# Softmax exponentials of VectorE placed in ScalarE's score groups, with three score banks on both sides and balanced PV batches

## The chip, the cores and the metric

One Trainium2 chip, one core. The metric is device time in microseconds of one execution of the kernel, as a median of several runs. In the rows, PE is TensorE (matmul), PEld its weight loads, DVE VectorE, ACT ScalarE, POOL GpSimd and SP SyncE, which issues most of the DMAs.

## What is computed

A transformer block with adaptive layer norm, for one sequence of 2048 tokens, width 640, 32 heads of 20, and a hidden width of 1536:

```python
mod = (silu(c) @ w_mod).reshape(1, 6, 1, -1)      # sa, ca, ga, sb, cb, gb
h = layernorm(x) * (1 + ca) + sa
q, k, v = split_heads(h @ wqkv)                    # 32 heads of 20
p = softmax(einsum('bhqd,bhkd->bhqk', q, k) * 20 ** -0.5)
x = x + ga * (merge_heads(einsum('bhqk,bhkd->bhqd', p, v)) @ wo)
h = layernorm(x) * (1 + cb) + sb
x = x + gb * (((h @ w_gate) * (h @ w_up)) @ w_down)
```

The 32 x 2048 x 2048 exponentials of the softmax are by far the most elementwise work.

## The kernel before

The program is planned before it is emitted. Every instruction is a `Task` with an engine, a guessed duration, dependences, a priority and slots to acquire (PSUM banks, SBUF buffers). `Sched.run` plays these tasks through guessed times, and what it picks, in the order it picks it, becomes the fixed order of each engine's queue; `emit_program` writes out the queues with semaphore waits. So a guessed duration (`ps_cost`, `sb_cost`, the numbers in `dve(...)` and `act(...)`) never sets a time on the chip, only the order.

**Units, items, chunks.** The queries are cut into four chunks of 512 (`CHUNKS`), the heads into eight sets of four. A chunk and a set are an item, 32 in all. An item has 64 units: one head of the four (its row strip `s`) times one key tile of 128. A unit's scores are one matmul of 32 rows by 512 columns (L919) into one PSUM bank; matmuls of different `s` run side by side in the four 32-row strips of TensorE.

**Two ways to the exponential.** 1824 units go through ScalarE: consecutive units form a group, alternately three in banks 0 to 2 (`GA`, set A) and two in banks 3 and 4 (`GB`, set B), and one `activation` (L944) takes the whole group to a slot of `PA` or `PB`. 224 units (`QUADS`: one quad of four units an item in the first chunk, two in the others) go through VectorE: the scores land in a bank of the pool `G` (banks 5 and 6), `P1` (L980) adds a bias, clamps at zero and writes int16 that is read as bf16, and five shifted copies of the quad (`SH`, L999) follow; the six versions are summed by the PV matmuls. `DB0` holds `NB0` quads, `DSS` holds `NSS` shifted copies.

**PV.** `pv_issue` writes matmuls of 128 rows by 32 columns (L1307): a unit's values against its exponentials, into the strip `s` of bank 7. A ScalarE unit has one, a VectorE unit six. At the end of an item VectorE transposes bank 7, normalizes, transposes back (L1050 to L1058), and DMAs (L1069) copy the pieces to `Ocp`.

**Other rounds on TensorE (X).** `Round` takes one bank of `G`, runs a chain of matmuls and releases the bank at its evacuation: K, Q and V projections (L738, L770), and for each finished chunk a `suffix`: output projection (op, L1119), layer norm and transposes (h2T, L1151), gate and up (L1191, 24 rounds of five), down (dn, L1221, eight rounds of twelve). `gate(...)` holds each suffix round back until the next chunk's groups have come so far; the last chunk's suffix is the tail. `xck` holds the chunk's residual, so it is reloaded (L1109) after the suffix before has written its output.

**What TensorE takes next** is decided in `pick_pe`: the next score group if its banks are free, with VectorE units' scores behind it when they are ready; then a PV batch of up to ten ScalarE units and whatever VectorE work is ready, from six matmuls on; then a VectorE unit's score by itself; then an X matmul; last a filler matmul, when planned activity in a window of 3.4 us is under `FILL_MIN`. TensorE, like the others, works its queue strictly in the order so found.

Of the kernel before, what the change touches and what calls it, by code (L numbers as in the profile page):

```python
# [55 lines left out]
class Slots:  # L56
# [6 lines left out]
    def avail(self):  # L63
        best = None
        for k, (i, rel) in enumerate(self.free):
            t = 0.0
# [23 lines left out]
class Sched:  # L90
# [83 lines left out]
    def acquire(self, task, t):  # L174
        got = []
        for pool, key, refs in task.acq:
            a = pool.avail()
            if a is None or a[0] > t:
                return False
        for pool, key, refs in task.acq:  # L180
            a = pool.avail()
# [167 lines left out]
SHIFTS = (0, 18, 34, 56, 77, 105)  # L349
SHIFT_GAIN = 3.046480226123085  # L350


def ps_cost(n):
    return n * 1.042 + 110.0
# [6 lines left out]
def build_kernel(nc, A_x, A_wqkv, A_wo, B_x, B_w_gate, B_w_up, B_w_down, c, w_mod, out):  # L361
# [94 lines left out]
    NPS = 4  # L456
    PA = alloc("PA", [128, NPS, 3 * 512], BF16)
    PB = alloc("PB", [128, NPS, 2 * 512], BF16)
    NB0, NSS = 2, 3
# [35 lines left out]
    NSX = 9  # L495
# [4 lines left out]
    GA = [0, 1, 2]  # L500
    GB = [3, 4]
# [4 lines left out]
    pA = Slots(list(range(NPS)), "PA")  # L506
    pB = Slots(list(range(NPS)), "PB")
# [142 lines left out]
    def ln1(tc, prio):  # L650
# [10 lines left out]
        for i in range(4):  # L661
            t = tc * 4 + i
            ags.append(dve(80, lambda e, t=t, i=i: e.bn_aggr(mv[:, t, :], st[:, i, :]), bns[2 * i:2 * i + 2], prio=prio))
# [10 lines left out]
        for i in range(4):  # L674
            t = tc * 4 + i
            t_xn[tc].append(dve(sb_cost(640, .27), lambda e, t=t, i=i: e.tensor_scalar(
                xn[:, s2, i, :], x0[:, t, :], mv[:, t, 0:1], rs[:, t:t + 1], op0=ALU.subtract, op1=ALU.mult),
                [p2] + dps, prio=prio))
# [3 lines left out]
    def hT_rounds(tc, prio):  # L682
# [3 lines left out]
        for k in range(KD):  # L686
# [6 lines left out]
            def after(r, k=k):  # L693
# [7 lines left out]
                return [dve(340, f, [r.last] + ev_col, prio=1)]  # L701
# [82 lines left out]
    units_per_chunk = [NSET * 4 * (NT * n // 512) for (_, n) in CHUNKS]  # L784
    act_units_per_chunk = [u - NSET * 4 * q for u, q in zip(units_per_chunk, QUADS)]
    gpc = [a / 2.5 for a in act_units_per_chunk]
    gstart = [sum(gpc[:i]) for i in range(NC + 1)]
# [78 lines left out]
    items = [(ci, j) for ci in range(NC) for j in range(NSET)]  # L866
    groups = []
    dquads = []
    pvq = []
    item_info = {}  # L870
    ubuf = []
    glist = []

    class Unit:
        __slots__ = ("item", "ci", "j", "s", "kts", "n", "task", "pslot", "off", "pv_ready", "is_d", "quad", "grp")

    for it, (ci, j) in enumerate(items):
        q0, n = CHUNKS[ci]
        rr = 512 // n
        nkg = NT // rr  # L880
        nq = QUADS[ci]
        info = {"pv_total": 0, "pv_done": 0, "acts": [], "quads": []}
        quads = [[] for _ in range(nq)]
        for kg in range(nkg):
            for s in range(4):
                u = Unit()
                u.item, u.ci, u.j, u.s, u.n = it, ci, j, s, n
                u.kts = list(range(kg * rr, kg * rr + rr))
                u.task = None
                u.quad = None  # L890
                q = kg // 4
                u.is_d = q < nq and s == kg % 4
                if u.is_d:
                    quads[q].append(u)
                else:
                    ubuf.append(u)
                    info["acts"].append(u)
        info["quads"] = quads
        for q in quads:
            dquads.append((it, q))  # L900
        item_info[it] = info
    gi_ = 0
    while ubuf:
        k = 3 if gi_ % 2 == 0 else 2
        glist.append(ubuf[:k])
        ubuf = ubuf[k:]
        gi_ += 1
    NG = len(glist)

# [15 lines left out]
    prev_s = [None]  # L925
    act_tasks = []
    for g, us in enumerate(glist):
        even = g % 2 == 0
        bset, banks_, pool_, pbuf = (setA, GA, pA, PA) if even else (setB, GB, pB, PB)
        ems = []  # L930
        deps = []
        for i, u in enumerate(us):
            deps += unit_score_deps(u)
            ems += unit_score_emits(u, (lambda b=banks_[i]: bank(b)))
# [4 lines left out]
        score_q.append((ts, us))  # L939
# [3 lines left out]
        def fexp(e, nu=nu, b0=banks_[0], pbuf=pbuf, cellp=cellp):  # L943
            return e.activation(pbuf[:, cellp["p"], 0:nu * 512],  # L944
                                ps[:, b0:b0 + nu, :].rearrange("p b c -> p (b c)"), AFT.Exp, scale=ESCALE)
        ta = Task("act", nu * 512 / 1.2 + 52.0, fexp, [ts], prio=g, name=f"E{g}")
        ta.acq = [(pool_, "p", nu)]

        def on_e(task, g=g, us=us, bset=bset, pool_=pool_, pbuf=pbuf, cellp=cellp):
            cellp["p"] = task.slots["p"]  # L950
            bset.done(0, task)
            sc.progress = max(sc.progress, g + 1)
            for i, u in enumerate(us):
                u.pslot = (pool_, pbuf, task.slots["p"])
                u.off = i * 512
                u.task = task
        ta.on_start = on_e
        sc.add(ta)
        act_tasks.append(ta)
        for u in us:  # L960
            pvq.append(u)

    st_pv = {"item": 0, "free": [d_pz]}
    dq_units = []
    d_state = {}
    pvd_ready = []
    for qi, (it, us) in enumerate(dquads):
        st_ = {"units": us, "p1": [], "slot": None, "item": it, "pv": [None] * NSH, "left": NSH, "rel": []}
        d_state[qi] = st_
        for x, u in enumerate(us):  # L970
            cell = {}
            ems = unit_score_emits(u, (lambda cell=cell: bank(cell["b"])))
            ts = Task("pe", 216.0, ems, list(dict.fromkeys(unit_score_deps(u))), ctr="pes", mode="S", name=f"D{qi}.{x}")
            ts.acq = [(G, "g", 1)]
            ts.on_start = lambda task, cell=cell: cell.__setitem__("b", task.slots["g"])
            sc.left += 1
            dq_units.append((ts, u, qi, x))

            def fp1(e, cell=cell, st_=st_, x=x):
                return e.tensor_scalar(DB0[:, st_["slot"], x * 512:(x + 1) * 512], bank(cell["b"]), EBIAS, 0.0,  # L980
                                       op0=ALU.add, op1=ALU.max)
            tp = Task("dve", ps_cost(512), fp1, [ts] + wpad[("K", 1)] + wpad[("Q", 1)] + st_["p1"][:1], prio=3.0 + .001 * qi,
                      name=f"P1.{qi}.{x}")
            if x == 0:
                tp.acq = [(sB0, "b0", NSH)]

            def on_p1(task, cell=cell, st_=st_, x=x):
                if x == 0:
                    st_["slot"] = task.slots["b0"]
                G.done(cell["b"], task)  # L990
            tp.on_start = on_p1
            sc.add(tp)
            st_["p1"].append(tp)
        st_["src"] = {0: st_["p1"]}
        for jj in range(1, NSH):
# [4 lines left out]
            tsx = Task("dve", sb_cost(2048, .27), fsh, list(st_["p1"]) + wpad[("K", 1)] + wpad[("Q", 1)], prio=2.5 + .001 * qi, name=f"SH.{qi}.{jj}")  # L1000
# [43 lines left out]
    def item_end_tasks(it):  # L1044
# [5 lines left out]
        t1 = Task("dve", ps_cost(n), lambda e: e.transpose(OT[:, 0:n], ps[:, BPV, 0:n]), [], prio=0.0, name=f"T1.{it}")  # L1050
        t1.acq = [(sOT, "o", 1)]
        item_info[it]["t1"] = t1
        t2 = dve(90, lambda e: e.reciprocal(invT[:, 0:nb32].unsqueeze(2),
# [4 lines left out]
        t4 = dve(sb_cost(n, .55), lambda e: e.transpose(OcT[:, cell["s"], 0:n], OTn[:, 0:n]), [t3], prio=1.5)  # L1058
# [29 lines left out]
    def suffix(ci):  # L1088
# [12 lines left out]
        def gate(w):  # L1101
            g = gb + 9 + int((gl - 9) * 0.985 * rc_[1] / w_tot)
# [11 lines left out]
        for tl in range(ntl):  # L1114
# [21 lines left out]
            ag = dve(85, lambda e, t=t, tl=tl: e.bn_aggr(mv2[:, t, :], st2[:, tl, :]), bn, prio=2.8)  # L1136
# [4 lines left out]
            t_xn2.append(dve(sb_cost(640, .27), lambda e, t=t, tl=tl: e.tensor_scalar(  # L1141
# [6 lines left out]
        for k in range(KD):  # L1148
# [6 lines left out]
            def after(r, k=k):  # L1155
                f = lambda e: e.tensor_scalar(h2T[:, k, 0:n], bankh(r.b["b"])[:, 0:n], mcol[:, 3, k:k + 1],  # L1156
                                              mcol[:, 2, k:k + 1], op0=ALU.mult, op1=ALU.add)
                return [dve(sb_cost(n, .55), f, [r.last, r_sb.evac[0], r_cb.evac[0]] + sfx_done.get("h2T", []) + proj_last,
# [81 lines left out]
    for it in range(len(items)):  # L1240
        ci, j = items[it]
        t1s[it] = item_end_tasks(it)
        if j == NSET - 1:
            sfx_done["qdead"] = [score_q[g][0] for g in range(NG) if any(u.ci == NC - 2 for u in score_q[g][1])][-1:] + \
                [a for (a, u, _, _) in dq_units if u.ci == NC - 2]
# [12 lines left out]
    PVMIN = 6  # L1258
    FILL_MIN = 3000.0
# [11 lines left out]
    def pv_candidates(t, maxn):  # L1271
# [24 lines left out]
        return res  # L1296

# [93 lines left out]
    def pick_pe(t):  # L1391
        sc.pull("pe")
        if pvstate["sidx"] < NG:
            ts, us = score_q[pvstate["sidx"]]
            if acquire_ready(ts, t):
                start = mode_start("S", t)
                dur, used = issue_S(ts, us, t, start)
                pvstate["sidx"] += 1
# [152 lines left out]
```

## Time and profile before

| | us |
|---|---|
| median of 3 runs | 1027.2 (1025.96 to 1028.4) |
| profiled execution | 1028.66 |
| its span, first to last instruction | 1026.6 |
| ScalarE busy / TensorE busy / VectorE busy | 856.0 / 940.6 / 598.8 |
| score matmuls L919, busy | 347.9 |
| VectorE's P1 L980 and shifts L999, busy | 145.2 and 184.6 |

Busy time of a group of instructions is the union of their spans; groups overlap. Matmul spans include the way through the array, so rows of different lines on TensorE add up to more than its busy time. A wait is told with the instruction that waited and the one that released it. In the chain of waits each piece is the work, or the wait, that the end of the kernel hung on at that moment.

### The profile page before, as it was taken

The page shows a single profiled execution, that of the slowest core. Times are in us where ns is not written, and L with a number is a line of the kernel's source. Part 1 is how long each engine was busy: PE and PEld are TensorE (multiplying, and loading weights), DVE is VectorE, ACT ScalarE, POOL GpSimd, SP SyncE. Part 2 cuts the span into 40 slices and gives each one's busy share as a digit, 9 for nine tenths or more (in the row PEclk, how much of TensorE's full clock was granted, in tenths as well). Part 3 has the DMA queues.
Part 4 walks back from the last instruction along what each step waited for, and adds up shares of the span by engine and source line. Part 5 has one row for each costly group of instructions (what it writes and reads, how often), then busy time and mean ns, then how long its engine had stood idle before and what let it go on. Part 6 is the DMA issues. An engine that isn't in the chain of part 4 may idle for free.

```text
span 1026.6 us, 16949 instructions
## 1 busy us (share of the span) xinstructions
PE 940.6 (92%) x7028; PEld 296.3 (29%) x7028; DVE 598.8 (58%) x1055; ACT 856.0 (83%) x758; POOL 57.5 (6%) x69
## 2 busy tenths in 40 slices
PE   2799999999998999999999889999999999999888
PEld 1342322222222222222223222222233322223545
DVE  5865555554459665545555676556466855664432
ACT  3277999999797899989999989899899989999010
POOL 5002000000016000000000010000000000000000
PEclk9899999999897898988899989989899979999989
DMA  9120000000050011110200101111441001111100
GB/s 306 52 65 4 4 4 5 3 2 4 4 145 4 3 42 30 36 24 4 43 17 11 36 5 36 43 30 23 86 85 44 4 23 30 43 37 42 55 1 26
DMA packets 82348, 37.46 MB, mean 36 GB/s; under 512 B 65632, under 2 KB 82272, under 8 KB 82272
## 3 DMA queue, kind: packets, MB, share of 16 engines
q1 hardware_dynamic: 79648, 33.11, 12.5%
q10 hardware_dynamic: 2624, 3.28, 1.0%
q8 instruction: 55, 0.90, 0.4%
q14 instruction: 21, 0.17, 0.1%
HBM read 31.13 MB, written 2.62 MB: 33 GB/s over the span
## 4 chain that ended last, share of the span: by engine, by line
PE 60%; DVE 18%; ACT 16%; issue 3%; POOL 1%; DMA 1%; ACTq 1%; DVEq 0%; POOLq 0%
PE ps_all L919 16%; PE ps_all L1307 13%; PE ps_all L1191 12%; ACT PA L944 9%; PE ps_all L738 8%; ACT PB L944 7%; DVE DSS L999 5%; PE ps_all L1221 4%; DVE DB L980 4%; PE ps_all L770 2%; PE ps_all L1119 2%; DVE st L657 1%; DVE OTn L1055 1%; DVE OT L1050 1%; DVE xck L1125 1%
## 5 line engine op out<-in xcount | busy, mean ns | idle before, releaser
L944 ACT ACTIVATE PA<-ps_all 128x1536 bf16<-128x1536 f32 x365 | 538.9, 1476 | 64.9 <-PE ps_all L919 63.2
L944 ACT ACTIVATE PB<-ps_all 128x1024 bf16<-128x1024 f32 x365 | 383.6, 1051 | 19.1 <-PE ps_all L919 18.6
L919 PE MATMUL ps_all<-QT,KT 32*128 32x512 bf16 x2048 | 347.9, 406 | 34.9 <-DVE DB L980 14.9
L999 DVE TENSOR_SCALAR DSS<-DB 128x2048 int16<-128x2048 int16 x280 | 184.6, 689 | 2.3 <-PE ps_all L1307 1.6
L919 PEld LDWEIGHTS ps_all<-QT,KT 32*128 32x128 bf16 x2048 | 83.5, 91 | 336.1 <-ACT PA L944 102.0
L1307 PE MATMUL ps_all<-PA,Vf 128*32 128x512 bf16 (+1 forms) x1095 | 165.9, 413 | 3.8 <-DVE OT L1050 3.7
L1307 PE MATMUL ps_all<-PB,Vf 128*32 128x512 bf16 (+1 forms) x729 | 160.5, 410 | 0.7 <-DVE OT L1050 0.4
L980 DVE TENSOR_SCALAR DB<-ps_all 128x512 int16<-128x512 f32 x224 | 145.2, 683 | 21.4 <-PE ps_all L919 19.5
L1307 PE MATMUL ps_all<-DSS,Vf 128*32 128x512 bf16 (+1 forms) x1120 | 146.7, 395 | 4.6 <-DVE DSS L999 4.5
L1191 PE MATMUL ps_all<-h2T,stg 128*128 128x512 bf16 x390 | 122.4, 420 | 0.5 <-DVE h2T L1156 0.3
L1206 DVE TENSOR_TENSOR hprod<-ps_all,gsb 128x512 bf16<-128x512 f32 x48 | 33.1, 690 | 82.9 <-PE ps_all L1191 82.9
L1196 DVE CAST gsb<-ps_all 128x512 bf16<-128x512 f32 x36 | 24.8, 690 | 80.1 <-PE ps_all L1191 80.1
L1221 PE MATMUL ps_all<-wd,hprod 128*128 128x320 bf16 x384 | 62.4, 304 | 0.8 <-DVE hprod L1206 0.8
L738 PE MATMUL ps_all<-hT,Wk 128*128 128x512 bf16 x160 | 50.3, 400 | 3.4 <-DVE QT L750 1.5
L1307 PEld LDWEIGHTS ps_all<-PA,Vf 128*32 128x32 bf16 (+1 forms) x1095 | 33.0, 95 | 64.0 <-issue 52.7
L1199 ACT CAST gsb<-ps_all 128x512 bf16<-128x512 f32 x12 | 7.0, 585 | 53.1 <-PE ps_all L1191 53.1
L1227 DVE TENSOR_TENSOR xck<-ps_all,xck 128x320 bf16<-128x320 f32 x32 | 15.6, 488 | 61.1 <-PE ps_all L1221 61.1
L1191 PEld LDWEIGHTS ps_all<-h2T,stg 128*128 128x128 bf16 x390 | 30.1, 101 | 68.5 <-issue 48.9
L738 PE MATMUL ps_all<-hT,Wq 128*128 128x512 bf16 x160 | 48.2, 397 | 0.0
L746 DVE CAST KT<-ps_all 128x512 bf16<-128x512 f32 x32 | 22.0, 688 | 42.2 <-PE ps_all L738 42.1
L750 DVE TENSOR_SCALAR QT<-ps_all 128x512 bf16<-128x512 f32 x32 | 22.1, 690 | 39.2 <-PE ps_all L738 39.2
L1307 PEld LDWEIGHTS ps_all<-PB,Vf 128*32 128x32 bf16 (+1 forms) x729 | 31.1, 95 | 47.3 <-issue 42.1
(69 smaller groups left out, 560.3 us busy)
## 6 DMA issues: line engine op xcount, KB each, us to landing
stg<-in_B_w_gate_dram SPq DMA_DIRECT2D x39, 160.0 KB, 2.4
stg<-in_B_w_up_dram SPq DMA_DIRECT2D x39, 160.0 KB, 2.7
x<-in_A_x_dram SPq DMA_DIRECT2D x4, 640.0 KB
xck<-in_A_x_dram SPq DMA_DIRECT2D x4, 640.0 KB
out_dram<-xck SPq DMA_DIRECT2D x16, 160.0 KB, 1.8
Ocp<-OcT SPq DMA_DIRECT2D x112, 20.0 KB
wd<-in_B_w_down_dram SPq DMA_DIRECT2D x1, 1920.0 KB, 8.9
wm<-in_w_mod_dram ACTq DMA_DIRECT2D x2, 800.0 KB, 8.7
```

The costliest lines, as they stand in the source:

```text
L738: f = lambda e, b, k=k: e.matmul(bank(b), wx[:, k, j, :], hT[:, k, tc * 512:(tc + 1) * 512], start=(k == 0), stop=(k == KD - 1))
L746: f = lambda e: e.tensor_copy(KT[:, j, tc * 512:(tc + 1) * 512], bank(r.b["b"]))
L750: f = lambda e, ci=ci, so=so, n=n: e.tensor_scalar(QT[ci][:, j, :], ps[:, r.b["b"], so:so + n], QSCALE, None, op0=ALU.mult)
L919: ems.append(lambda e, i=i, kt=kt: e.matmul(dstf()[:, i * u.n:(i + 1) * u.n], KT[32 * u.s:32 * u.s + 32, u.j, kt * 128:(kt + 1) * 128], QT ...
L944: return e.activation(pbuf[:, cellp["p"], 0:nu * 512], ps[:, b0:b0 + nu, :].rearrange("p b c -> p (b c)"), AFT.Exp, scale=ESCALE)
L980: return e.tensor_scalar(DB0[:, st_["slot"], x * 512:(x + 1) * 512], bank(cell["b"]), EBIAS, 0.0, op0=ALU.add, op1=ALU.max)
L999: return e.tensor_scalar(DSS[:, cell["s"], :], DB0[:, st_["slot"], :], float(SHIFTS[jj]), None, op0=ALU.add)
L1191: f = lambda e, b, k=k, cell=wbuf[w_]: e.matmul(ps[:, b, 0:n], cell["t"][:, k, :], h2T[:, k, 0:n], start=(k == 0), stop=(k == KD - 1))
L1196: f = lambda e: e.tensor_copy(gsb[:, gs, 0:n], ps[:, r.b["b"], 0:n])
L1206: f = lambda e: e.tensor_tensor(hprod[:, fc, 0:n], ps[:, r.b["b"], 0:n], gsb[:, gs, 0:n], ALU.mult)
L1221: f = lambda e, b, fc=fc, tl=tl, hf=hf: e.matmul(ps[:, b, 0:320], hprod[:, fc, tl * 128:(tl + 1) * 128], wd_sb[:, fc, 320 * hf:320 * hf + ...
L1307: ems.append(lambda e, i=i, kt=kt, stt=stt, stp=stp: e.matmul(ps[32 * s:32 * s + mc, BPV, 0:u.n], Vf[:, (kt * H + 4 * u.j + s) * VW:(kt * ...
```

## The change

1. `glist` is formed anew. Set A stays three banks wide, set B is two wide in the first chunk and three in the last three (`WIDE`), where it takes bank 5 from `G` (`widen`). Where a group is three wide and a VectorE unit is due (`due`, with a lead of `D_LEAD` = 0.35 of an item, and never among the first 18 ScalarE units), the group is two ScalarE units and that VectorE unit, of another row strip. The separate list of VectorE scores (`dq_units`), their place in `pick_pe` and `d_ok` are gone.
2. The bank set of such a group has two holders, the exponential and P1, and is free when both are done. The first unit of a quad makes the score group acquire the `DB0` slot. P1 has priority 0.8 in place of 3.0.
3. `PA` and `PB` (four slots each) become one ring `PP` of eight slots of three units. `NB0` goes from 2 to 3, `NSS` from 3 to 2.
4. `pick_pe`: an X matmul comes ahead of PV when planned activity is low and the ring is not; PV takes up to 24 candidates, cut by `pv_balance` to nearly equal numbers in the four strips, from 8 matmuls on right after a score group and 12 otherwise (or when forced by a low ring or an item's end); then X; then small PV batches.
5. Planner constants: `ps_cost`, the durations of layer norm, evacuations, shifts and transposes; `NSX` 11; `GATE_F` (0.985 for the three gated suffixes, as before). `gstart` and `gpc` are counted from `glist`.

`CHUNKS`, `QUADS` and the `suffix` work are as before. The diff, cut to its core:

```diff
+D_LEAD = 0.35
+NB0, NSS = 3, 2
+NPS = 8
+WIDE = (1, 2, 3)
+PVMIN, PVMAX, PVCAP = 8, 12, 24
...
-    PA = alloc("PA", [128, NPS, 3 * 512], BF16)
-    PB = alloc("PB", [128, NPS, 2 * 512], BF16)
-    NB0, NSS = 2, 3
+    PP = alloc("PP", [128, NPS, 3 * 512], BF16)
...
-    while ubuf:
-        k = 3 if gi_ % 2 == 0 else 2
-        glist.append(ubuf[:k])
...
+    while ap < NA or dp < len(dlist):
+        even = len(glist) % 2 == 0
+        wide = 3 if even or ap >= NA or ubuf[ap].ci in WIDE else 2
+        us = ubuf[ap:ap + wide]
+        d = None
+        if not quad_left and dp < len(dlist):
+            quad_left = dlist[dp:dp + 4]
+        if wide == 3 and quad_left and due[dp] <= ap:
+            two = ubuf[ap:ap + 2]
+            for u in quad_left:
+                if u.s not in [v.s for v in two]:
+                    d, us = u, two
+                    break
...
+        glist.append((us, d, 0 if even else 3, wide))
...
-        ts.acq = [(bset, "b", 1)]
+        ts.acq = [(bset, "b", 1 if du is None else 2)]
+        if g in widen:
+            ts.acq.append((G, "g5", 1, 5))
...
+            if du.first:
+                ts.acq.append((sB0, "b0", NSH))
...
+            tp = Task("dve", ps_cost(512), fp1, [ts] + wpad[("K", 1)] + wpad[("Q", 1)], prio=0.8, name=f"P1.{qi}.{x}")
+            tp.on_start = lambda task, bset=bset: bset.done(0, task)
...
+    def pv_balance(cands, force):
...
+        m = max(len(l) for l in aa)
+        if not force:
+            best = 0
+            for k in range(1, m + 1):
+                if sum(min(len(l), k) for l in aa) >= 0.85 * 4 * k:
+                    best = k
+            m = best
...
+        if sc.recent(t) < FILL_MIN and len(pP.free) >= RINGLOW and pick_x(t):
+            return True
+        cands = pv_candidates(t, PVCAP)
...
+            cands = pv_balance(cands, force)
+            nwork = sum(1 if k == "a" else 4 for k, _ in cands)
+            if cands and (nwork >= (PVMIN if just_s[0] else PVMAX) or force):
...
+        if pick_x(t):
+            return True
+        if cands and not js and len(cands) >= 2:
+            pv_issue(cands, t)
+            return True
```

More of the change, by code (lines that the diff above doesn't have):

```diff
@@ L61, in __init__, with avail @@
         self.hold = {}
-    def avail(self):
+    def avail(self, only=None):
         best = None
         for k, (i, rel) in enumerate(self.free):
+            if only is not None and i != only:
+                continue
             t = 0.0
@@ L505, in build_kernel @@
     setB = Slots([0], "B")
-    pA = Slots(list(range(NPS)), "PA")
-    pB = Slots(list(range(NPS)), "PB")
+    pP = Slots(list(range(NPS)), "PP")
     sB0 = Slots(list(range(NB0)), "B0")
@@ L782, in v_round @@
         proj_last.append(r.last)
[L784 to L787, printed above, removed]
+    items = [(ci, j) for ci in range(NC) for j in range(NSET)]
+    groups = []
+    dquads = []
+    pvq = []
+    item_info = {}
+    ubuf = []
+    glist = []
+    class Unit:
+        __slots__ = ("item", "ci", "j", "s", "kts", "n", "task", "pslot", "off", "pv_ready", "is_d", "quad", "grp", "first")
@@ new lines, in build_kernel @@
+    for it, (ci, j) in enumerate(items):
+        q0, n = CHUNKS[ci]
+        rr = 512 // n
+        nkg = NT // rr
+        nq = QUADS[ci]
+        info = {"pv_total": 0, "pv_done": 0, "acts": [], "quads": []}
+        quads = [[] for _ in range(nq)]
+        for kg in range(nkg):
+            for s in range(4):
+                u = Unit()
+                u.item, u.ci, u.j, u.s, u.n = it, ci, j, s, n
+                u.kts = list(range(kg * rr, kg * rr + rr))
+                u.task = None
+                u.quad = None
+                q = kg // 4
+                u.is_d = q < nq and s == kg % 4
+                if u.is_d:
+                    quads[q].append(u)
+                else:
+                    ubuf.append(u)
+                    info["acts"].append(u)
+        info["quads"] = quads
+        for q in quads:
+            dquads.append((it, q))
+        item_info[it] = info
@@ L789, in build_kernel @@
+    NG = len(glist)
+    gstart = []
+    for ci in range(NC):
+        gstart.append(min(g for g in range(NG) if any(u.ci == ci for u in glist[g][0])))
+    gstart.append(NG)
+    gpc = [gstart[i + 1] - gstart[i] for i in range(NC)]
+    widen, narrow = set(), set()
+    bw = 2
+    for g in range(1, NG, 2):
+        w = glist[g][3]
+        if w > bw:
+            widen.add(g)
+        if w < bw:
+            narrow.add(g)
+        bw = w
     for tc in range(4):
@@ L924, in build_kernel @@
     score_q = []
-    prev_s = [None]
     act_tasks = []
-    for g, us in enumerate(glist):
-        even = g % 2 == 0
-        bset, banks_, pool_, pbuf = (setA, GA, pA, PA) if even else (setB, GB, pB, PB)
+    act_of = {}
+    st_pv = {"item": 0, "free": [d_pz]}
+    d_state = {}
+    for qi, (it, us) in enumerate(dquads):
+        d_state[qi] = {"units": us, "p1": [None] * 4, "slot": None, "item": it}
+        for x, u in enumerate(us):
+            u.quad = (qi, x)
+    for g, (us, du, b0, wide) in enumerate(glist):
+        bset = setA if b0 == 0 else setB
@@ L957, in build_kernel @@
[L957 to L966, printed above, removed]
-    for qi, (it, us) in enumerate(dquads):
[L968 to L993, printed above, removed]
```

256 lines of the change are left out of this document (124 added, 132 removed).

## Prediction

> **What bounds the kernel now.** I read the page's first two parts, then the busy times by stage, the waits, and the chain of waits at both ends.
>
> ```profile
> PE 940.6 (92%) x7028; PEld 296.3 (29%) x7028; DVE 598.8 (58%) x1055; ACT 856.0 (83%) x758; POOL 57.5 (6%) x69
> ...
> ACT  3277999999797899989999989899899989999010
> ...
> PEclk9899999999897898988899989989899979999989
> ```
>
> Neither TensorE's 92% nor ScalarE's 83% settles it: matmul ends are modelled, and ScalarE stands near nine tenths in some slices and at zero at the end. So next ScalarE's exponentials (L944) alone, by stage: the head, then the four query chunks, then the tail.
>
> ```profile
> core 0: us, ACT busy (x), PEclk, DMA share, GB/s
> 30.00:100.00 70.00, 40.83 (x36) 0.93 0.08 26
> 100.00:272.00 172.00, 164.23 (x144) 0.97 0.01 4
> 272.00:498.00 226.00, 205.46 (x178) 0.88 0.13 33
> 498.00:713.00 215.00, 201.93 (x176) 0.92 0.12 28
> 713.00:949.00 236.00, 227.11 (x199) 0.94 0.19 43
> ...
> 250.00:275.00 25.00, 17.82 (x17) 0.80 0.02 5
> ...
> 325.00:350.00 25.00, 17.95 (x16) 0.66 0.02 4
> ...
> 525.00:550.00 25.00, 24.95 (x23) 1.00 0.05 17
> ```
>
> Columns: the stretch, its length, ScalarE's busy time and instructions, the granted TensorE clock. At clock 1.00 ScalarE is never idle (24.95 of 25); at 0.80 and 0.66 it loses 7 of 25. How fast it can go is in the order of instructions in time:
>
> ```profile
> 30.29 1.45 ACT L944 ACTIVATE PA<-ps_all 128x1536 bf16<-128x1536 f32 x1 [5.13 <-PE ps_all L919]
> ...
> 55.07 1.49 ACT L944 ACTIVATE PA<-ps_all 128x1536 bf16<-128x1536 f32 x1
> 56.40 1.07 ACT L944 ACTIVATE PB<-ps_all 128x1024 bf16<-128x1024 f32 x1
> 57.30 1.51 ACT L944 ACTIVATE PA<-ps_all 128x1536 bf16<-128x1536 f32 x1
> ...
> 948.09 0.65 ACT L944 ACTIVATE PB<-ps_all 128x512 bf16<-128x512 f32 x1
> ```
>
> Start to start, a group of three units takes 1.33 us and one of two 0.90, so a pair takes 2.23 and one exp on average 1.115. The 365 pairs need 814 us, and run from 30.3 to 948.7, 918.4 us: **104 us are lost.** By stage (elapsed less count times 1.115): head 29.9, first chunk 11.4, second 27.5, third 18.8, fourth 14.1, in all 101.7 (exps on a border count twice). Who ended those waits:
>
> ```profile
> PEld ps_all L919 <- DVE DB L980: 58.7, 122, 1.3
> ACT PA L944 <- PE ps_all L919: 63.2, 49, 15.7
> ACT PB L944 <- PE ps_all L919: 18.6, 15, 4.7
> ```
>
> ScalarE waits for score matmuls only. Its three-bank group waits more: the scores that refill it have only the two-bank exp (0.90) to hide under. So the phase is ScalarE's work, plus the times TensorE brings scores late. After it comes a tail of 78 us, last below.
>
> **The change part by part.**
>
> *ScalarE's work.* All 224 VectorE units leave the G banks and take the third bank of an exp group. Forming the groups by the new rule gives 206 groups for the first chunk and 170 or 171 for each later one, 717 against 730; 390 of them carry three ScalarE units and 327 two (1824 units, as before). That is 390 x 1.33 + 327 x 0.90 = 813 us against 814: **-1**. The change removes no exponential work; it can only win lost time.
>
> *TensorE's work.*
>
> ```profile
> 498.00:713.00 215.00, 202.03 (x1564) 59.41 (x1565) 129.80 (x227) 201.93 (x176) 4.04 (x8) 0.92 0.12 28
> ...
> 498.00:713.00 215.00, 87.15 (x504) 20.95 (x502) 0.92 0.12 28
> ...
> 498.00:713.00 215.00, 74.34 (x801) 17.88 (x804) 0.92 0.12 28
> ...
> 90.23 0.76 PE ps_all L1307 x9
> ...
> 91.31 0.54 PE ps_all L1307 x7
> ...
> 93.26 0.32 PE ps_all L919 x3
> ```
>
> The first three rows are the third chunk's stage: all engines (TensorE, weight loads, VectorE, ScalarE, GpSimd), then TensorE on the score line L919 alone, then on the PV line L1307 alone. The last three are pieces of the chain. A score group takes 0.32 however many row strips it uses. A PV batch pays by its fullest column strip: 7 matmuls are two deep, 0.54; 9 are three deep, 0.76. A balanced batch of 12 is also three deep, so 0.063 us a matmul, against 74.34/801 = 0.093 now. Scores: 171 groups x 0.32 = 55 us in place of 87, since a VectorE unit's matmul now runs beside its group's two others. PV: 801 x 0.063 / 0.92 = 55 in place of 74. TensorE's need falls from 202 to about 151 us of 215. The group itself needs a bank more per pair; its scores now hide under 1.33 instead of 0.90 wherever the other group is three wide.
>
> How much lost time comes back? At half clock TensorE supplied about half of ScalarE's pace (202 x 0.92 x 2 = 372 us of need for 176 x 1.115 = 196 of exps, 0.53); with 151 it supplies 0.71, so the shortage shrinks from 0.47 to 0.29, a factor of 0.6. The stalls at full clock, from the narrow cover, mostly go, and projection and suffix rounds come ahead of small PV batches, which takes away part of what starts a slow stretch (the 7 us at 250 to 275). I take one half in all four chunks: 11.4+27.5+18.8+14.1 = 71.8, half is **-36**. Ends: 0, and -72 if no stall remained. The end -72 is out of reach for one reason in the rows:
>
> ```profile
> L999 DVE TENSOR_SCALAR DSS<-DB x280: 626/682/1890, 37.8 to 932.2; 128x2048 int16<-128x2048 int16 x140
> ...
> L863 POOL TENSOR_TENSOR wd<-wd,gab x12: 1387/1395/1845, 303.3 to 324.9; 128x640 bf16<-128x640 bf16 x12
> ...
> 315.85 1.89 DVE L999 TENSOR_SCALAR DSS<-DB 128x2048 int16<-128x2048 int16 x1
> ...
> core 0: 1026.6 us, clock 0.928
> ```
>
> A shift copy (minimum/median/maximum in ns) takes 0.68 us, but the one at 315.85, while GpSimd scales w_down (303 to 325), takes 1.89; that stays, and DSS goes from three buffers to two. The last row is span and mean granted clock.
>
> The Trainium skill (TensorE: Matmul & The Clock Gate, Terms) prices a throttled stretch at its length times the clock's missing share. By the Trainium skill's rule the mean clock of 0.928 would be worth 0.072 x 1026.6 = 74 us, an estimate, and the sum would end near 950 if the change kept the clock full. The rows bear out that idle time and low clock go together, not that the change lifts the clock, so the sum stays with -36.
>
> *Head.* VectorE units now wait until 18 ScalarE units have gone. VectorE's two lines for them used:
>
> ```profile
> 30.00:100.00 70.00, 5.16 (x8) 0.93 0.08 26
> ...
> 30.00:100.00 70.00, 6.60 (x10) 0.93 0.08 26
> ```
>
> These are L980 and L999, 11.8 us of which part moves out of the layer-norm queue. Ends 0 and -11.8; I take **-5**, nearer the lower, since the work still falls inside the head in part.
>
> *Tail.*
>
> ```profile
> 949.40 10.17 PE ps_all L1221 x74
> ...
> 960.12 1.79 DMA out_dram<-xck
> ...
> 961.92 4.30 DMA xck<-in_A_x_dram
> 966.26 5.26 PE ps_all L1119 x25
> ...
> 955.01 0.74 SPq L1069 DMA_DIRECT2D Ocp<-OcT  x1
> ...
> DMA to landing us min/median/max: 1.7/1.7/1.7
> ```
>
> When the last exp ends, 74 matmuls of the third suffix's down projection are still queued, as other rounds came last on TensorE; then xck is written out and reloaded before the last output projection starts at 966.26. Its other input, the last Ocp piece, has landed at 955.01 + 0.74 + 1.7 = 957.45. If the backlog is gone by then, the start moves to 8.7 us after the last exp instead of 17.5: **-8.8**. Ends 0 and -8.8; I take all of it, because about 50 us of freed TensorE time per chunk is far more than 10. The 60.4 us from there on keep their instructions.
>
> *Edits at nothing.* New cost constants, `Slots.avail(only)` and moved code alter only the order that is written out. NSX 11 changes no load: nsx is the smaller of it and 24576/2560 = 9. PP has 8 slots for 20 to 24 units where PA and PB held 20. CHUNKS and QUADS stay.
>
> *New waits.*
>
> ```profile
> L980 DVE TENSOR_SCALAR DB<-ps_all 128x512 int16<-128x512 f32 x224 | 145.2, 683 | 21.4 <-PE ps_all L919 19.5
> ...
> 936.10 1.18 PE ps_all L1191 x5
> ```
>
> A set that held a VectorE unit is refilled only after its P1 (L980, 0.68) as well as its exp; and the first unit of a quad makes the score group wait for a DB0 slot. Both now stand in front of all of TensorE's queue. After a two-unit exp (0.90) and a three-unit one of the other set (1.33), P1 has 2.23 - 0.68 less about 0.6 for refilling (0.32 of scores and the hand-overs, an estimate), some 0.9 us, before ScalarE feels it (0.5 where both are two wide). I take 0. Ends: 0, and the 58.7/122 = 0.48 us that TensorE waits for L980 now, on all 224: +107. Rounds in the last three chunks have one G bank instead of two shared with the VectorE units. A gate round then cycles in about 1.2 (936.10 above) + 0.7 (an evacuation of 512 columns, as L980) + 0.4 us (a score group between), and 45 rounds fill some 110 us of a chunk's 200: 0.
>
> **Sum.** 1026.6 - 1 - 36 - 5 - 8.8 = 976 of span. That execution took 1028.66, 2.1 more than its span and 1.5 over the median of 1027.2; so 977 on the median's scale.
>
> **The rivals.**
>
> *The clock eats it.* TensorE is less busy, idles more often, gets half clock oftener, and stalls as much as now; only tail, head and -1 remain: 1027 - 15 = 1012. For it: clock and idle time go together in the stage rows. Against: the matmul work per exp is the same and the pace no slower. The Trainium skill speaks for it (TensorE: Matmul & The Clock Gate, A second HAM failure mode: psum-queue depth-cycling): idling briefly between groups that cycle through banks makes the clock swing; the trace agrees as far as the 0.80 and 0.66 above stand beside idle ScalarE. Chance 0.20.
>
> *Slower: P1 holds the score banks.* VectorE runs in order, its evacuations wait for TensorE rounds, and P1 behind them is late; TensorE stands at the score group, ScalarE drains. It decides where the mean delay over the 224 groups passes 51/224 = 0.23 us beyond the slack; at 0.48 the time is 977 + 107 = 1084, at 0.35 about 1055. For it: the 58.7 us; VectorE's load rises from 60% (129.80 of 215) to about 65%. Against: the slack of 0.5 to 0.9, and P1 now goes before nearly all else on VectorE. Chance 0.11.
>
> *The single G bank starves the suffix.* Rounds slip as before, the tail keeps its 17.5, or grows by a few rounds of 2.3: 977 + 9 to + 25, some 995. Against: the 110 of 200 us. Chance 0.06.
>
> **How the numbers follow.** Forecast 0.63, at 977, its own range 958 to 998 (three quarters to one quarter of the 72 regained). The clock rival 0.20 (of it 0.02 within 0.2%), the bank rival 0.06, the slower one 0.11. About 0.2% is what a measurement of this kernel tells from no change. Faster 0.87, same 0.02, slower 0.11. For 8 in 10 the range takes the forecast, the bank rival and most of the clock rival: 954 to 1015; left out are the slower case and the ends.
>
> **What would show it.** Right: some 717 exps, the last ending near 905; TensorE rows at L919 near 235 us in all; no exp waiting over 2 us after 110 us except around the w_down scaling; the first L1119 of the tail within 10 us of the last exp. Wrong: long waits of scores for DB, a granted clock well under 0.93, or suffix matmuls left over at the last exp.

## The result, and the profile after

The changed kernel takes 962.4 us (median of four runs, 957.5 to 962.7) against 1026.6: a ratio of 0.9375, interval 0.9334 to 0.9416. The forecast was 977, in a range of 954 to 1015. The profiled execution of the changed kernel is its shortest run, 957.5 with a span of 955.6, so its trace shows 71 us less span where the medians differ by 64.

Lines shift in the new kernel: L944 (exponentials) is L996, L919 (scores) L958, L980 (P1) L1023, L999 (shifts) L1036, L1307 (PV) L1363, L1119 L1157, L1191 L1229, L1221 L1259, the filler L1475 L1528. First, ScalarE's exponentials by stage; the stages end where the new chunks do.

```profile
core 0: us, ACT busy (x), PEclk, DMA share, GB/s
30.00:100.00 70.00, 51.61 (x48) 0.95 0.08 26
100.00:272.00 172.00, 170.92 (x160) 0.99 0.09 24
272.00:477.00 205.00, 200.52 (x170) 0.98 0.13 30
477.00:682.00 205.00, 202.47 (x171) 0.98 0.12 29
682.00:889.00 207.00, 204.55 (x172) 0.95 0.21 45
```

Idle time of ScalarE is length less busy time. In the head it fell from 29.2 to 18.4 us, in the four chunks from 7.8, 20.5, 13.1 and 8.9 to 1.1, 4.5, 2.5 and 2.5. The chain of waits says the same in one line: the shares of the span by engine, before and then after.

```profile
PE 60%; DVE 18%; ACT 16%; issue 3%; POOL 1%; DMA 1%; ACTq 1%; DVEq 0%; POOLq 0%
```

```profile
ACT 50%; PE 36%; issue 7%; DVE 5%; DMA 2%; POOL 0%; SPq 0%; ACTq 0%; POOLq 0%
```

The end hung on TensorE and VectorE for four fifths of the time before; now ScalarE's own work is half of it. Who waits for scores, who for P1, and span and granted clock:

```profile
PEld ps_all L958 <- ACT PP L996: 272.2, 585, 1.2
DVE DB L1023 <- PE ps_all L958: 94.2, 87, 6.1
ACT PP L996 <- PE ps_all L958: 33.2, 19, 10.9
PEld ps_all L958 <- DVE DB L1023: 1.7, 4, 0.5
...
core 0: 955.6 us, clock 0.969
```

The arrow has turned. Before, TensorE waited for P1 122 times, 58.7 us in all; now 4 times, 1.7 us, and P1 waits for scores instead. These are waits of TensorE's weight loads; the array itself stood idle for less of that time, as a row further down shows. TensorE now waits more for ScalarE's exponentials (272.2 us, before 102.0 and 88.5 for its two lines), which is what a kernel bound by ScalarE looks like. The clock rose from 0.928 to 0.969.

The tail, from the chain of waits: start, length, what.

```profile
890.80 0.73 DVE OT L1088
...
894.86 0.71 SPq L1107
895.61 1.92 DMA Ocp<-OcT
897.57 0.87 PE ps_all L1157 x5
```

The last exp ends at 889.1 and the output projection starts 8.5 us later, released by the last Ocp piece and no longer by the reload of xck.

### The profile page after: what moved, and what is told of

Same layout as the page of the kernel before. It is cut to its first block, busy times and chain, and to the rows that moved or that the text cites. A ratio compares the mean times of both kernels' runs of the same rounds, so it can differ in the third digit from the quotient of the medians.

```text
span 955.6 us, 17031 instructions
## 1 busy us (share of the span) xinstructions
PE 855.0 (89%) x7060; PEld 275.1 (29%) x7060; DVE 594.6 (62%) x1055; ACT 846.6 (89%) x745; POOL 58.2 (6%) x69
## 4 chain that ended last, share of the span: by engine, by line
ACT 50%; PE 36%; issue 7%; DVE 5%; DMA 2%; POOL 0%; SPq 0%; ACTq 0%; POOLq 0%
ACT PP L996 49%; PE ps_all L958 9%; PE ps_all L1363 8%; PE ps_all L743 7%; PE ps_all L1229 4%; PE ps_all L775 3%; PE ps_all L1259 2%; DMA wkq<-in_A_wqkv_dram 2%; DVE DSS L1036 1%; PE ps_all L1528 1%; PE ps_all L1157 1%; DVE xck L1163 0%; DVE st L662 0%; PE ps_all L1189 0%; PE ps_all L694 0%
## 5 line engine op out<-in xcount | busy, mean ns | idle before, releaser
L996 ACT ACTIVATE PP<-ps_all 128x1536 bf16<-128x1536 f32 (+1 forms) x717 | 830.2, 1358 | 34.5 <-PE ps_all L958 33.2
L958 PE MATMUL ps_all<-QT,KT 32*128 32x512 bf16 x2048 | 286.7, 393 | 58.9 <-ACT PP L996 54.4
L1023 DVE TENSOR_SCALAR DB<-ps_all 128x512 int16<-128x512 f32 x224 | 153.3, 685 | 95.4 <-PE ps_all L958 94.2
L1036 DVE TENSOR_SCALAR DSS<-DB 128x2048 int16<-128x2048 int16 x280 | 188.2, 693 | 24.1 <-PE ps_all L1363 22.7
L1363 PE MATMUL ps_all<-PP,Vf 128*32 128x512 bf16 (+1 forms) x1824 | 176.2, 397 | 0.5 <-DVE OT L1088 0.3
L958 PEld LDWEIGHTS ps_all<-QT,KT 32*128 32x128 bf16 x2048 | 69.6, 91 | 308.2 <-ACT PP L996 272.2
L1229 PE MATMUL ps_all<-h2T,stg 128*128 128x512 bf16 x390 | 113.9, 384 | 2.0 <-DVE hprod L1244 0.7
L1363 PE MATMUL ps_all<-DSS,Vf 128*32 128x512 bf16 (+1 forms) x1120 | 101.5, 390 | 3.2 <-DVE DSS L1036 2.7
L1259 PE MATMUL ps_all<-wd,hprod 128*128 128x320 bf16 x384 | 68.0, 305 | 0.9 <-DVE hprod L1244 0.8
L1363 PEld LDWEIGHTS ps_all<-PP,Vf 128*32 128x32 bf16 (+1 forms) x1824 | 41.2, 94 | 93.5 <-issue 86.2
L1229 PEld LDWEIGHTS ps_all<-h2T,stg 128*128 128x128 bf16 x390 | 30.0, 97 | 64.9 <-issue 35.7
L1259 PEld LDWEIGHTS ps_all<-wd,hprod 128*128 128x128 bf16 x384 | 32.0, 98 | 33.7 <-issue 21.7
L1363 PEld LDWEIGHTS ps_all<-DSS,Vf 128*32 128x32 bf16 x1120 | 28.9, 96 | 27.1 <-DVE DSS L1036 12.4
L751 DVE CAST KT<-ps_all 128x512 bf16<-128x512 f32 x32 | 21.9, 686 | 20.6 <-PE ps_all L743 20.5
```

The source lines that it names most:

```text
L958: ems.append(lambda e, i=i, kt=kt: e.matmul(dstf()[:, i * u.n:(i + 1) * u.n], KT[32 * u.s:32 * u.s + 32, u.j, kt * 128:(kt + 1) * 128], QT ...
L996: return e.activation(PP[:, cellp["p"], 0:nu * 512], ps[:, b0:b0 + nu, :].rearrange("p b c -> p (b c)"), AFT.Exp, scale=ESCALE)
L1036: return e.tensor_scalar(DSS[:, cell["s"], :], DB0[:, st_["slot"], :], float(SHIFTS[jj]), None, op0=ALU.add)
L1229: f = lambda e, b, k=k, cell=wbuf[w_]: e.matmul(ps[:, b, 0:n], cell["t"][:, k, :], h2T[:, k, 0:n], start=(k == 0), stop=(k == KD - 1))
L1259: f = lambda e, b, fc=fc, tl=tl, hf=hf: e.matmul(ps[:, b, 0:320], hprod[:, fc, tl * 128:(tl + 1) * 128], wd_sb[:, fc, 320 * hf:320 * hf + ...
L1363: ems.append(lambda e, i=i, kt=kt, stt=stt, stp=stp: e.matmul(ps[32 * s:32 * s + mc, BPV, 0:u.n], Vf[:, (kt * H + 4 * u.j + s) * VW:(kt * ...
```

## The experiments

Two theories stood at the start: the gain is in the score groups (riding, that is a VectorE unit in the third place of a group, or the third bank of set B), or in PV, the order of X, and the planner's durations. The first four runs each undo one part of the change.

**Set B two wide.**

```diff
-WIDE = (1, 2, 3)
+WIDE = ()
```

> The changed kernel with set B two banks wide in all four chunks (WIDE empty); VectorE units still ride, in set A alone, and G keeps both its banks. Cover theory (the third bank of set B gains the time, because the scores of each group then hide under an exp of 1.33 us instead of 0.90): the stalls of ScalarE come back in part, 15 to 25 us slower than 962, and long waits of L996 for L958 at full clock. Riding theory (the gain is that a VectorE unit's scores no longer take TensorE time and G banks of their own): within 5 us of 962, with L958's busy time still under 300 us.

970.6 us, ratio 0.9447 (0.9408 to 0.9485), 8 us slower than the whole change and between the two theories; L958 is busy 320.7 us, over the 300 of the riding theory. Where did the 8 go? The groups of L996 (count, busy time, mean ns, idle time before), of the change and of this kernel:

```profile
L996 ACT ACTIVATE PP<-ps_all 128x1536 bf16<-128x1536 f32 (+1 forms) x717 | 830.2, 1358 | 34.5 <-PE ps_all L958 33.2
```

```profile
L996 ACT ACTIVATE PP<-ps_all 128x1024 bf16<-128x1024 f32 (+1 forms) x819 | 841.3, 1173 | 30.3 <-PE ps_all L958 27.4
```

ScalarE does not idle more (30.3 us before its exps, 34.5 after the change). It has 819 instructions instead of 717 and is busy 841.3 instead of 830.2, 0.11 us for each of the 102 more. The third bank pays by larger groups, not by cover.

**PV not balanced.**

```diff
-            cands = pv_balance(cands, force)
```

> The changed kernel without the call of pv_balance: a PV batch takes all candidates that are ready, up to 24 and in their own order, with the same least sizes. PV theory (balanced batches free TensorE, as my prediction's 19 us a chunk had it): PV's cost per matmul rises, L1363 is busier by 20 us or more, and the time is 10 to 20 us longer. Score theory (the gain is in the score groups; the trace of after has PV at 85 ns a matmul start to start, before 88): within 4 us of 962.

956.0 us, ratio 0.9317 (0.9285 to 0.9348): not slower, if anything faster, but the intervals overlap. TensorE on the PV line in the third chunk's stage, with balance and then without, and the clock without:

```profile
477.00:682.00 205.00, 68.58 (x827) 16.27 (x827) 0.98 0.12 29
```

```profile
477.00:682.00 205.00, 81.84 (x843) 20.47 (x843) 1.00 0.12 28
...
core 0: 954.9 us, clock 0.989
```

Balance does save TensorE 13 us in this stage, but on an engine that is no longer the bound, and the clock is higher without it (0.989 against 0.969).

**The old order of PV and X.**

```diff
-        if sc.recent(t) < FILL_MIN and len(pP.free) >= RINGLOW and pick_x(t):
-            return True
...
-PVMIN, PVMAX, PVCAP = 8, 12, 24
+PVMIN, PVMAX, PVCAP = 6, 6, 24
```

> The changed kernel with the old order between PV and the X rounds: no X matmul ahead of PV when activity is low, and PV batches from six matmuls on (cap 24 and balance kept). Order theory (projection and suffix rounds in time keep the clock full and empty the tail): suffix matmuls are left over at the last exp, the granted clock falls from 0.97 towards 0.93, and the time rises by 15 to 30 us. Score theory: the exp phase stays within 8 us, only the tail grows, by at most 9 us.

955.2 us, ratio 0.9314 (0.9277 to 0.9350). Neither the tail nor the clock suffers (0.979; the last output projection starts 7.3 us after the last exp): the order theory falls.

**The old durations in the planner** (all of the diff's changed numbers in `dve(...)`, `ps_cost` and the `Task` durations set back).

> The changed kernel with the planner's old durations (110 ns fixed cost of a PSUM read, layer norm, shifts, transposes and evacuations as before); no instruction is added or removed, only the written order can differ. Planner theory (the written order fits the chip better with measured durations, which is where the stalls went): 15 us or more slower, with waits of TensorE for VectorE. Score theory: within 5 us of 962.

959.7 us, ratio 0.9351 (0.9310 to 0.9391): the same. The planner theory falls for the changed kernel.

So no single part but riding was left. The next runs take it alone, and approach it from the kernel before.

**Riding alone** (the four edits above together, with PVCAP 10 and the old rule that an item also counts as ending when fewer than PVMIN of its ScalarE units are ready).

> Only the riding of VectorE units in the three-wide groups is left of the change (with its ring PP and the buffer counts 3 and 2): set B is two wide everywhere, PV is not balanced and goes by the old sizes (from 6, up to 10 candidates), no X matmul comes ahead of PV, and the planner has its old durations. Riding theory: most of the gain stays, 965 to 985 us, L958 busy near 300 us. Sum theory (each part holds up the others, so that taking one alone away shows little, but taking all away does): 1000 us or more.

979.6 us, ratio 0.9522 (0.9484 to 0.9560): about three quarters of the gain stay. The other parts together are worth some 17 us, though singly they showed -7 to 8. ScalarE's busy time is 864.6 us here and 846.6 in the whole change, so the 17 us show up there. Set B alone accounts for 11 of these 18 (857.7 in its run), because a VectorE unit in a group takes the place of a ScalarE unit and the groups become more: 819 in place of 717. Which of the other parts has the rest is not shown. The clock was higher than in any other profile, 0.991. The exps from 100 us on, and the waits for P1:

```profile
100.00:910.00 810.00, 798.07 (x773) 1.00 0.13 32
...
PEld ps_all L958 <- DVE DB L1023: 2.5, 6, 0.5
```

From 100 us to the last exp TensorE had the full clock, hardly a wait for P1 was left, and still the kernel took 17 us more than the change.

**The kernel before, three banks on both sides.**

```diff
     GA = [0, 1, 2]
-    GB = [3, 4]
-    G = Slots([5, 6], "G")
+    GB = [3, 4, 5]
+    G = Slots([6], "G")
...
-        k = 3 if gi_ % 2 == 0 else 2
+        k = 3
...
-    PB = alloc("PB", [128, NPS, 2 * 512], BF16)
+    PB = alloc("PB", [128, NPS, 3 * 512], BF16)
...
     def d_ok(qi, x):
-        return d_state[qi]["item"] <= st_pv["item"] + 1
+        if d_state[qi]["item"] > st_pv["item"] + 1:
+            return False
+        a = sB0.avail() if x == 0 else (0.0, 0)
+        return a is not None and a[0] <= sc.t
```

> The kernel before with three score banks on both sides in all four chunks, nothing riding; G keeps one bank, which the VectorE units and all rounds share (the planner takes a quad's first score only when a DB0 slot is free). Cover theory: the longer cover of 1.33 us takes the stalls away, 1005 us or less. Riding theory: the scores of VectorE units still need their own turn and bank, now the only one, so no gain: 1020 us or more, with TensorE waiting for DB more than 59 us.

1228.4 us, ratio 1.1932 (1.1887 to 1.1976).

```profile
PEld ps_all L919 <- DVE DB L980: 111.6, 153, 1.9
...
core 0: 1229.1 us, clock 0.829
```

The waits for P1 nearly double and the clock falls to 0.829. Of the 202 us of span some 120 are lost up to the last exp (1068.4 against 948.7), and 83 behind it, where no VectorE score is left: the third suffix's rounds are still to be done. Two things are mixed here, the third bank and the single G bank, so the run does not test the longer cover by itself; it shows that VectorE's scores and all rounds do not get by with one G bank.

**The kernel before, VectorE's scores only beside a group.**

```diff
-        if pvstate["didx"] < len(dq_units):
+        if pvstate["didx"] < len(dq_units) and (min(len(pA.free), len(pB.free)) < RINGLOW or pvstate["sidx"] >= NG):
             td, u, qi, x = dq_units[pvstate["didx"]]
```

> The kernel before, but a VectorE unit's score is taken only right behind a score group, in another row strip, and by itself only when a ring is low or no group is left; it still lies in a G bank. TensorE-time theory (the separate turns of those scores, 0.32 us and more each, are what TensorE lacked): 1015 us or less, fewer score turns. Bank theory (their wait for G banks and P1 is what stops the queue, wherever they are issued): within 6 us of 1027 or slower, with TensorE still waiting some 50 us for DB.

967.6 us, ratio 0.9391 (0.9346 to 0.9436). One condition in the planner, no bank moved, gives nearly the whole gain. (A VectorE score may still go by itself when a ring is low or no group is left.)

```profile
PEld ps_all L919 <- ACT PA L944: 124.1, 281, 1.2
...
PEld ps_all L919 <- DVE DB L980: 0.2, 1, 0.2
...
L919 PE MATMUL ps_all<-QT,KT 32*128 32x512 bf16 x2048 | 290.1, 390 | 32.9 <-ACT PA L944 20.3
```

The waits for P1 are gone, L919 is busy 290 us in place of 348. The two-bank set and its cover of 0.90 us are as before. Both theories of this run had a half of it: the turns are gone, and so are the waits, which the bank theory had wrongly kept. What those turns looked like is in the kernel before, in order of time:

```profile
526.91 3.20 DVE L980 TENSOR_SCALAR DB<-ps_all 128x512 int16<-128x512 f32 x5
527.05 0.40 PE L1307 MATMUL ps_all<-DSS,Vf 128*32 128x512 bf16 x4 [0.20 <-DVE DSS L999]
527.38 1.25 PE L919 MATMUL ps_all<-QT,KT 32*128 32x512 bf16 x7
...
528.85 0.87 PE L919 MATMUL ps_all<-QT,KT 32*128 32x512 bf16 x4 [0.21 <-DVE DB L980]
```

For 2.3 us TensorE does nothing but eleven score matmuls, at the pace of VectorE's P1 (five in 3.20), since each VectorE unit needs a bank that the P1 before must free; PV and X are queued behind. The rows show what the turns look like, not what they cost: ScalarE's groups lose next to nothing in this very stretch.

**The kernel before, VectorE's scores with a margin.** To part the wait from the turn:

```diff
     def d_ok(qi, x):
-        return d_state[qi]["item"] <= st_pv["item"] + 1
+        if d_state[qi]["item"] > st_pv["item"] + 1:
+            return False
+        a = G.avail()
+        return a is not None and a[0] <= sc.t - 800.0
```

> The kernel before, but the planner takes a VectorE unit's score, alone or behind a group, only when a G bank has been free for 0.8 us of planned time, so that a P1 that is late on the chip no longer stops TensorE's queue; the scores still take turns of their own. Wait theory (what cost the kernel before its time is TensorE standing at such a score until P1 frees a bank): 975 us or less, near the 967.5 of the run with scores beside groups only, and TensorE's waits for DB under 15 us. Turn theory (the turns themselves, 0.32 us each, are the cost): 1005 us or more, though the waits for DB are gone.

982.2 us, ratio 0.9567 (0.9511 to 0.9623): between the two theories and outside the ranges of both, nearer to the wait. The first row below is the kernel before, the others are this one.

```profile
PE ps_all L919 <- DVE DB L980: 14.9, 44, 0.8
...
PEld ps_all L919 <- DVE DB L980: 0.8, 1, 0.8
PE ps_all L919 <- DVE DB L980: 0.5, 1, 0.5
...
L919 PE MATMUL ps_all<-QT,KT 32*128 32x512 bf16 x2048 | 334.1, 389 | 18.4 <-ACT PA L944 11.8
...
core 0: 981.1 us, clock 0.976
```

The waits are gone: 0.8 us of weight loads, where it was 58.7, and 0.5 of idle array, where it was 14.9 (the two overlap, so they are not added). The turns stay: L919 is busy 334 us. Counted in the traces, the scores that start 0.1 us or more apart from every other score are 188 before, 168 here, 11 in the run with scores beside a group and 13 in the change.

Against before, taking the waits away gives 4.3%; taking the turns away too gives 6.1%; the whole change 6.25%. So about 44 of the 64 us go with the waits, some 15 to 18 with the turns, and the rest of the change is hardly to be told from nothing on top. Part of both is won in the tail: the last output projection starts 17.5 us after the last exp before, 11.4 here, 7.2 beside a group, 8.5 in the change. The split compares whole written orders, since either condition also moves what is written after a score; no run takes out the waits and leaves the order as it was.

Riding alone has neither the waits nor the turns, and yet took 12 us more than the scores beside a group: ScalarE was busy 864.6 us there and 848.5 beside a group, with 819 groups against 730. So riding by itself makes the groups of ScalarE smaller, and the third bank makes up for it. The two kernels also differ in their rings and buffer counts (`PP`, `NB0`, `NSS`), which no run takes alone.

**P1 late.** In the changed kernel, P1's priority back from 0.8 to `3.0 + .001 * qi`.

> The changed kernel with the old priority of P1 on VectorE (3.0 in place of 0.8): evacuations, shifts and layer norm are written ahead of it. Bank theory, the slower rival of the prediction (a set that holds a VectorE unit is refilled late): 10 us or more slower than 962, with waits of L958 for DB. Slack theory (P1 has 0.5 to 0.9 us to spare): within 5 us of 962.

977.4 us, ratio 0.9530 (0.9482 to 0.9578).

```profile
PEld ps_all L958 <- DVE DB L1023: 14.0, 29, 0.8
```

The prediction's slower rival is real in kind: 15 us when P1 is written late. With P1 first it costs 1.7 us of waits.

**A better version?** Three tries, on the reading that ScalarE is now the bound: more work for VectorE, and the two edits that had come out lowest.

Two quads an item in the first chunk as well:

```diff
-QUADS = [1, 2, 2, 2]
+QUADS = [2, 2, 2, 2]
```

> The changed kernel with two quads an item for VectorE in the first chunk too (QUADS 2,2,2,2): 32 units fewer for ScalarE. If ScalarE's own work is now the bound, the time falls by up to 32 x 0.427 = 14 us, to 950. If VectorE, with 8 quads of some 6.2 us more beside the projections' evacuations, becomes the bound of the first chunk, it stays at 962 or rises, with scores waiting for DB.

967.2 us, ratio 0.9389 (0.9352 to 0.9427): no gain. The last exp ends at 894 instead of 889. The stage of the first chunk, in the change and then here (TensorE, weight loads, VectorE, ScalarE, GpSimd):

```profile
100.00:272.00 172.00, 166.36 (x1237) 48.36 (x1234) 89.49 (x143) 170.92 (x160) 2.96 (x3) 0.99 0.09 24
...
100.00:272.00 172.00, 172.00 (x1370) 50.16 (x1362) 122.95 (x203) 162.03 (x159) 0.00 (x0) 1.00 0.02 4
```

ScalarE's busy time falls by 9 us in this stage, and by 6 in the head (45.2 against 51.6), so the 14 us are lost there. TensorE has no idle time left in the stage, VectorE has 49 us: a unit that moves to VectorE brings six PV matmuls in place of one. That TensorE is the limit there is likely, and not shown by a run of its own.

The edits of "PV not balanced" and "the old order" together:

> The changed kernel without pv_balance, without X ahead of PV, and with PV from six matmuls on (cap 24): the two edits that were faster one by one (956.0 and 955.2). If they win different stalls, 950 to 953; if both remove the same ones (less slow clock in the exp phase, 3 and 24 us of it against 38), 954 to 957.

957.9 us, ratio 0.9337 (0.9296 to 0.9378): they do not add up, and it can't be told from the change.

That kernel with three quads an item in the last chunk (`QUADS = [1, 2, 2, 3]`):

> The kernel of e15 with three quads an item for VectorE in the last chunk (QUADS 1,2,2,3): 32 units fewer for ScalarE, 8 quads of some 6.2 us more for VectorE. If ScalarE's own work is the bound and VectorE (about 65 percent busy there) has room, up to 14 us faster than e15. If VectorE fills up, P1 frees the score banks late: the time is that of e15 or longer, with waits of L958 for DB.

965.3 us, ratio 0.9407 (0.9353 to 0.9460). Its chain of waits has why:

```profile
883.28 13.23 PE ps_all L1259 x96
897.05 1.78 DMA out_dram<-xck
898.84 4.34 DMA xck<-in_A_x_dram
903.22 3.73 PE ps_all L1157 x15
```

The last exp ends 11 us earlier, at 878, but the whole down projection of the third suffix is left over, and the tail's old chain through xck is back. The gain is lost again in the tail. None of the kernels is told apart from the change as faster.

## Why the prediction was right, and where it was not

- **ScalarE's work, -1.** Right: 717 exps, from 30.0 to 889.1 us. Of these 859.1 us, 813 are work, so 46 are lost in place of 104.
- **Lost time, -36 and head -5.** Right in kind, too small: 58 us came back instead of 41. The term that was mis-sized is the share of one half for the four chunks. Counted as the sum counts it, start to start, the time lost there fell from 71.8 to some 26 us, so nearly two thirds came back. The half was worked out as if most stretches at half clock stayed, with ScalarE only better supplied in them; in the trace's clock they fell from 126 to 41 us of the four chunks. The head gave some 10 us, near its end of 11.8, instead of 5. The term's own range was also added up wrongly: three quarters and one quarter of 72 lead to 959 and 995, not 958 and 998.
- **"At clock 1.00 ScalarE is never idle"** was read from one stretch of 25 us. Before, about half of the time lost in the four chunks lay at full clock, and riding alone lost some 41 us there with no half clock at all.
- **Tail, -8.8.** Right: the start of the last output projection is 8.5 us after the last exp, forecast 8.7. The rest from there took 58.0 instead of 60.4. The reason given, some 50 us of freed TensorE time a chunk, is not borne out (next point), and the backlog also went in the kernel before with scores beside a group, which has the old order and the old PV batches.
- **TensorE's need.** The forecast of 151 us for the third chunk's stage stood on scores (87 to 55) and PV (74 to 55). The whole stage and its scores:

```profile
477.00:682.00 205.00, 183.67 (x1627) 55.13 (x1624) 136.53 (x236) 202.47 (x171) 4.33 (x8) 0.98 0.12 29
...
477.00:682.00 205.00, 68.60 (x513) 16.65 (x510) 0.98 0.12 29
```

  Scores took 69, PV 69 and TensorE was busy 184 of 205: this step failed in its sizes. Over the whole kernel the scores took 286.7 us where 235 had been named as a sign. Busy spans count the way through the array (a score matmul's span is 393 ns on average, a turn 0.32 us), which my price by start to start did not. It failed in its weight too: the PV part, 19 of the 51 us that I credited, cost no time when undone alone. And I named the stalls' cause wrongly: I put them on the narrow cover of 0.90 us and TensorE's load, where the runs show VectorE's scores, by their waits and their turns: with both gone and the narrow cover left in place the kernel took 967.6. I had quoted the row of the waits, 58.7 us, and used it only as a danger of the new waits.
- **New waits at 0.** Right: 1.7 us, with a single G bank that held no suffix back (the third suffix's down projection ended at 878.8, ahead of the last exp). It was forecast by slack, and the slack is there only when P1 is written first: 14.0 us of waits when it is late.
- **The clock rival.** Wrong way round: the clock rose. The Trainium skill (TensorE: Matmul & The Clock Gate, A second HAM failure mode: psum-queue depth-cycling) gave it support; the trace agrees in part: of two kernels with the same score groups the less busy TensorE has the lower clock (0.969 balanced, 0.989 unbalanced), but from before to after TensorE's busy time fell from 940.6 to 855.0 us and the clock rose. By the Trainium skill (TensorE: Matmul & The Clock Gate, Terms) an estimate of the gain from a full clock was 74 us; 0.969 would be worth 42 of it. How much of the gain the clock carried, and how much of the clock merely followed from the missing stalls, these runs don't part. They do show that a full clock is not enough (riding alone, 979.6), and that the half clock still left in the change costs little: without balance it falls from 41 to 3 us of the four chunks, and the time lost there only from some 26 to 23.
- **What was luck.** The mechanism of the sum's largest term, a TensorE with 51 us less to do in each chunk, is not what the runs show. That the time still fell into the range owes something to the half having been taken broadly, between nothing and all of the lost time.

## What to carry to other kernels

An engine's queue is worked in order, so a cheap instruction that waits for a slower engine's buffer stops all the work behind it: look in the waits for what the busiest engine waits for, and try moving that one instruction first. Here one planner condition gave nearly what a new bank layout, a balance and an order gave together. When the bound moves (here to ScalarE), savings on the old bound buy little, and what is won by moving work off the new one can be lost at the next limit, here the tail and the first chunk.

## What was not expected of the hardware

Less TensorE work went with a lower granted clock: 0.969 with balanced PV (68.6 us of it in a stage), 0.989 without (81.8), with the same work for ScalarE. The other variants of the change line up alike: TensorE was busy 854 to 859 us at 0.969 to 0.979, 878 to 898 at 0.984 to 0.989, and 923 at 0.991 with riding alone. The kernel before does not fit the line, with 940.6 us at 0.928. The runs don't show which of the two is cause.
